# adaLN, S4D convolution and SwiGLU on one core: x normalised once as whole rows, the skip term as a matrix product, a new order of instructions

## The chip, the cores and the metric

The kernel runs on one core of one Trainium2 chip. The metric is the device time of one execution in microseconds (us). The engines are TensorE (PE; its weight loads are listed as PEld), VectorE (DVE), ScalarE (ACT), GpSimd (POOL) and SyncE (SP), which here only issues DMA transfers. SBUF and PSUM are the two on-chip memories; x, the weights and the kernel's scratch tensors lie in DRAM.

## The reference

One sequence x of L = 2048 rows and D = 640 channels passes a modulated block. All numbers are f32.

```python
mod = (silu(c) @ w_mod).reshape(6, 640)          # sa, ca, ga, sb, cb, gb
h = layernorm(x) * (1 + ca) + sa
K[d, l] = 2 * Re(sum_n C[d, n] dt[d] * exp(A[d, n] dt[d] l))     # N = 128
y = irfft(rfft(K, 2L) * rfft(h.T, 2L))[:, :L].T + h * D_skip
x = x + ga * y
h = layernorm(x) * (1 + cb) + sb
x = x + gb * ((silu(h @ w1) * (h @ w3)) @ w2)    # F = 1728
```

## The kernel before, in words

**Work and stages.** The 640 channels are five blocks of 128, numbered 0 to 4, and b is such a block below. For each of them three things are made.

- *The convolution's kernel K.* `gen_tasks` and `gen_chunk` make it in 8 chunks of 16 channels, 40 chunks in all. A chunk takes GpSimd (phases `ph`, three operations on sizes, `yy` and `xx`), ScalarE (sines `tr`, in PSUM), VectorE (five multiplications of `yy` and `xx` with `tr`) and TensorE (64 small products into the PSUM tile `kps`). ScalarE then copies `kps` to `ks` in SBUF. `skip` (L1761) adds D_skip, held in `dsk`, to column 63 of each of the chunk's four groups in `ks`; column 63 is where the time slot t = 0 lies.
- *The input h.* `h_tasks` makes it in four tiles of 128 partitions by 4 rows by 128 channels. `h_load` fetches a tile of x with four DMAs of 64 KB into `xq` (SBUF). `h_norm` (L1639) normalises it with four 128x128 operations, one per row slot, on ScalarE or VectorE, from `xq` into a PSUM bank `hn`. `h_mul` (L1650) multiplies by the row rA and `h_add` (L1654) adds rB, both on VectorE with one 128x512 operation; the first works in place in `hn`, the second writes `hb` (SBUF). `h_store` writes `hb` to the DRAM tensor `hs`, from where `h_fetch` brings it back transposed as `xb`.
- *The spectra.* `first_tasks` is the first stage of the transform: TensorE products `ps`, of `xb` for h and of `ks` for K, copied by ScalarE or VectorE to `sp`. `spectra_tasks` is the second stage: products `fh` and `fk` with the table `wb`, VectorE's complex product `fp`, the first stage back `fz`, copied to `zt` and stored in DRAM as `zd`.

`tail_tasks` follows: the last stage back, x + ga*y, the second LayerNorm, transposes, and the first products `gu` of the feed-forward. `ffn` does the rest of the feed-forward. Its instructions stand outside the plan described below, at lines such as L665 and L841.

**What comes before the blocks** (`early_tasks`, L2000). x is loaded whole, as four tiles `xs` with four DMAs of 320 KB each, and its statistics are taken on ScalarE (sums, squares) or VectorE. The squares are written over `xs`, which nothing needs afterwards. `hscale` makes the reciprocal deviations. The modulations sa, ca and ga are made as rows: five products `mr`, from 960 KB loads of w_mod, are spread over the partitions, copied to three rows `rw`, and folded by two 128x640 operations into rA = (1 + ca)*ga and rB = sa*ga (L2114), so that ga is already in h. Then SP loads the 2 MB table `wb`. sb, cb and gb are made in columns, from five more 960 KB loads of w_mod, `c0` to `c4`, into `xs_w` tiles that share the four buffers of `xs`. Their last product leads to `cols` and to an event called `inv`. At `inv` the buffers `xs` are closed and others opened; the loads of h for blocks 1 to 4 and the second spectra wait for it.

**What sets the order.** The class `Plan` (L168) holds the tasks. Each has an engine (or a choice of two), an assumed duration, the tasks that it waits for, buffers that it takes and gives, and a rank. A list scheduler goes through them with a model of the engines, and where several tasks are ready on one engine, the lowest rank goes first. `RANKS` (L34) is a list of numbers, one for each task up to the last spectra, found by a search that was run beforehand; the tasks of `tail_tasks` have ranks written in the code. The resulting order is then fixed for each engine, so each engine runs its queue in order and a waiting instruction holds up all behind it. The assumed durations therefore decide the order and nothing else. Tasks with `port=True` are placed so that VectorE and GpSimd don't run them side by side; the five multiplications of a chunk, `h_mul` and `h_add` haven't got that mark.

**How to find things in the profile.** Everything that is ordered by the plan has one line there, L157, in which the instruction is recorded; tiles tell the operations apart. The numbers of the tiles are left out, so that `sp<-ps` is any copy of the first stage and `kps<-yy,xx` the products of any chunk.

Of the kernel before, what the change touches and what calls it, by code (L numbers as in the profile page):

```python
# [10 lines left out]
F32 = mybir.dt.float32  # L11
# [7 lines left out]
P = 128  # L19
# [262 lines left out]
class K:  # L282
# [132 lines left out]
    def h_stats(self, xs, b):  # L415
# [10 lines left out]
        def squares(j):  # L426
            s = slice(4 * b + j, 4 * b + j + 1)
            nc.scalar.activation(xs[:, j], xs[:, j], AF.Square, bias=self.h_nm[:, s], accum_out=self.h_ss[:, s])
# [1571 lines left out]
    def early_tasks(self, e):  # L2000
# [122 lines left out]
        def load_w(k):  # L2123
            w[k] = self.mod_load_rows(k, 1)
# [51 lines left out]
```

## Time and profile before

| what | value |
|---|---|
| median of 3 runs | 973.41 us (972.67 to 974.10) |
| profiled execution, its own time | 972.31 us |
| its span, first to last instruction | 970.5 us |
| mean granted TensorE clock | 0.975 of full speed |
| TensorE busy | 859.9 us, 89% of the span, 7985 products |
| VectorE busy | 702.0 us, 72% |
| ScalarE busy | 546.4 us, 56% |
| GpSimd busy | 340.5 us, 35% |
| DMA | 127.31 MB, mean 131 GB/s |

The page of the profile shows one execution. A row of busy tenths divides the span into 40 equal slices, one digit for each: 9 means 90% busy or more. The row GB/s shows what the DMA engines moved in a slice. A group's row has the line, the engine, the operation, "out<-in" by tiles, the shape (partitions x elements) and the count, then the busy time in us, the mean duration in ns, and the idle time of the engine just ahead of such instructions with what ended it. A row of the timeline begins with the start in us from the span's start and the duration in us. A row of windows has the window, its length, and then for PE, PEld, DVE, ACT and POOL the busy time with the number of instructions, the granted clock, the DMA share and the GB/s.

### The profile page before, as it was taken

The page shows a single profiled execution, that of the slowest core. Times are in us where ns is not written, and L with a number is a line of the kernel's source. Part 1 is how long each engine was busy: PE and PEld are TensorE (multiplying, and loading weights), DVE is VectorE, ACT ScalarE, POOL GpSimd, SP SyncE. Part 2 cuts the span into 40 slices and gives each one's busy share as a digit, 9 for nine tenths or more (in the row PEclk, how much of TensorE's full clock was granted, in tenths as well). Part 3 has the DMA queues.
Part 4 walks back from the last instruction along what each step waited for, and adds up shares of the span by engine and source line. Part 5 has one row for each costly group of instructions (what it writes and reads, how often), then busy time and mean ns, then how long its engine had stood idle before and what let it go on. Part 6 is the DMA issues. An engine that isn't in the chain of part 4 may idle for free.

```text
span 970.5 us, 20551 instructions
## 1 busy us (share of the span) xinstructions
PE 859.9 (89%) x7985; PEld 681.8 (70%) x7985; DVE 702.0 (72%) x1395; ACT 546.4 (56%) x1022; POOL 340.5 (35%) x371
## 2 busy tenths in 40 slices
PE   1464787889899997899999999999999999999997
PEld 1132665767778884677777778888788888888775
DVE  7998899999999968886767677557456464645422
ACT  6877788979888851564434455346444344443412
POOL 1797889879799600002111111000011212120000
PEclk9996999999999999799999999999999999999999
DMA  9955453723425268935434422276342322220374
GB/s 218 275 168 191 111 136 95 177 66 106 111 80 152 74 159 206 241 118 182 122 120 139 122 96 68 82 209 194 112 134 64 102 77 86 82 82 28 108 220 133
DMA packets 110506, 127.31 MB, mean 131 GB/s; under 512 B 10568, under 2 KB 90696, under 8 KB 109128
## 3 DMA queue, kind: packets, MB, share of 16 engines
q1 hardware_dynamic: 109032, 125.21, 45.3%
q8 instruction: 63, 1.03, 0.5%
q10 hardware_dynamic: 1376, 0.79, 0.3%
q14 instruction: 35, 0.29, 0.1%
HBM read 95.82 MB, written 30.15 MB: 130 GB/s over the span
## 4 chain that ended last, share of the span: by engine, by line
PE 70%; DVE 17%; ACT 5%; issue 4%; DMA 3%; POOL 1%; SPq 1%; ACTq 0%; DVEq 0%
PE c L157 19%; PE acc L157 18%; PE X L157 12%; PE ps L157 4%; PE gu L157 3%; DVE yy L157 3%; PE kps L157 3%; PE fz L157 2%; PE fk L157 2%; DVE fp L157 2%; PE fh L157 2%; DVE hn L157 2%; DVE xx L157 2%; DVE xb L157 1%; ACT tr L157 1%
## 5 line engine op out<-in xcount | busy, mean ns | idle before, releaser
L157 PE MATMUL acc<-ah,w 128*128 128x512 f32 x560 | 173.2, 395 | 2.4 <-DMA w<-w2d 1.7
L157 PEld LDWEIGHTS acc<-ah,w 128*128 128x128 f32 x560 | 103.7, 188 | 26.4 <-issue 2.1
L157 PE MATMUL acc<-al,w 128*128 128x512 f32 x260 | 102.4, 394 | 0.0
L665 DVE TENSOR_TENSOR wl<-s,wh 128x256 fp32r<-128x256 f32 x92 | 38.9, 423 | 67.5 <-ACT wh L664 67.1
L841 POOL TENSOR_TENSOR s<-wr 128x256 f32<-128x256 f32 x22 | 16.4, 744 | 187.8 <-DMA wr<-in_w 94.8
L157 POOL TENSOR_TENSOR ph<-p,p 128x1024 int32<-128x1024 int32 x40 | 79.2, 1979 | 8.2 <-ACT tr L157 8.0
L664 ACT ACTIVATE wh<-s 128x256 fp32r<-128x256 f32 x92 | 37.6, 410 | 78.5 <-PE X L157 58.1
L157 PE MATMUL kps<-yy,xx 128*32 128x64 f32 x2560 | 51.8, 234 | 28.6 <-DVE xx L157 21.4
L157 DVE TENSOR_TENSOR yy<-yy,tr 128x512 f32<-128x512 f32 (+1 forms) x80 | 75.3, 943 | 1.2 <-ACT tr L157 0.6
L157 PEld LDWEIGHTS kps<-yy,xx 128*32 128x32 f32 x2560 | 45.1, 116 | 38.3 <-issue 22.0
L664 ACT ACTIVATE wh<-wr 128x256 fp32r<-128x256 f32 x92 | 38.4, 418 | 56.0 <-PE X L157 42.3
L842 POOL TENSOR_TENSOR s<-s,wr 128x256 f32<-128x256 f32 x22 | 16.6, 755 | 134.0 <-issue 133.9
L902 ACT ACTIVATE t<-g 128x512 f32<-128x512 f32 x44 | 27.8, 632 | 52.7 <-DVE g L866 52.7
L157 ACT ACTIVATE tr<-ph,hpi 128x512 f32<-128x512 f32 x80 | 54.6, 690 | 4.4 <-DVE xx L157 2.7
L157 PEld LDWEIGHTS acc<-al,w 128*128 128x128 f32 x260 | 48.9, 188 | 10.8 <-DVE al L665 0.3
L871 DVE SCALAR_TENSOR_TENSOR g<-t,g 128x512 f32<-128x512 f32 x48 | 33.7, 702 | 31.3 <-ACT t L902 29.3
L157 POOL TENSOR_TENSOR yy<-e,e 128x512 f32<-128x512 f32 x48 | 52.4, 1109 | 8.8 <-PE kps L157 5.9
L157 DVE TENSOR_TENSOR xx<-tr,xx 128x512 f32<-128x512 f32 x80 | 54.3, 680 | 1.1 <-ACT tr L157 1.1
L157 PE MATMUL ps<-wk,ks 128*64 128x128 f32 x640 | 42.4, 285 | 13.6 <-DVE ks L157 8.9
L157 ACT ACTIVATE tr<-ph 128x512 f32<-128x512 int32 x80 | 47.3, 598 | 12.4 <-DVE yy L157 6.5
L157 PE MATMUL ps<-wk,xb 128*64 128x128 f32 x640 | 46.1, 295 | 6.3 <-ACT sp L157 3.0
L157 PEld LDWEIGHTS ps<-wk,ks 128*64 128x64 f32 x640 | 37.0, 143 | 20.3 <-ACT hn L157 6.6
(448 smaller groups left out, 2379.7 us busy)
## 6 DMA issues: line engine op xcount, KB each, us to landing
w<-w2d SPq DMA_DIRECT2D x42, 640.0 KB, 3.9
wr<-in_w SPq DMA_DIRECT2D x50, 320.0 KB, 3.9
zd<-zt SPq DMA_DIRECT2D x40, 256.0 KB, 2.9
w2d<-w SPq DMA_DIRECT2D x14, 640.0 KB, 3.5
xs<-in_x SPq DMA_DIRECT2D x16, 320.0 KB, 11.3
hs<-hb SPq DMA_DIRECT2D x20, 256.0 KB, 2.5
xb<-hs SPq DMA_DIRECT2D x20, 256.0 KB, 4.9
iz<-zd SPq DMA_DIRECT2D x32, 160.0 KB, 5.0
```

The source lines that it names most:

```text
L157: self.prev = self.k.order(f(*a, **kw), self.prev)
L664: self.nc.scalar.activation(H, v, AF.Copy)
L665: eng.tensor_tensor(Lo, v, H.bitcast(F32), op=ALU.subtract)
L841: eng.tensor_tensor(s[0], u[:, 0:2], u[:, 2:4], op=ALU.add)
L842: eng.tensor_tensor(s[1], s[0], g[:, 0:2], op=ALU.subtract)
L871: V.scalar_tensor_tensor(g, th, 1.0, g, op0=ALU.add, op1=ALU.mult)
L902: tanh = lambda o, i: A.activation(o, i, AF.Tanh, scale=0.5)
```

## The change

- `squares` writes its result to a spare tile `junk`, so that `xs` keeps x.
- New tasks `zn` normalise each of the 16 row slots of `xs` in place, once `hscale` is done, with one 128x640 operation on ScalarE or VectorE (`norm_rows`). Four new DMA tasks `zo` store the four tiles, 1.3 MB each, in a new DRAM tensor `zs`.
- `h_load` of the blocks 1 to 4 fetches its tile from `zs` with one DMA of 256 KB, and waits for its `zo`; block 0 has no load and reads `xs` directly. `h_norm` and its PSUM bank are gone: `h_mul` reads `xq` (block 0: `xs`) and writes `xq`, in SBUF. The buffers of `xs` are given free by `zo` and by `h_mul` of block 0, not by the squares.
- `skip` is gone. After the 64 products of a chunk, one more product, of the 128x128 identity `ident` with the chunk's 128x4 of `dsk`, is added to column 63 of each group of `kps`. The copy to `ks` follows as before. The first stage waits for that copy (`r`) in place of the addition (`d`), and a chunk's products wait for the copy of two chunks before.
- `h_make`, which nothing called, is deleted.
- Many assumed durations are changed, also of tasks in `tail_tasks`, and `RANKS` is new throughout. Some waits for the last of eight tasks are written as waits for all eight.

```diff
+        self.zs = d.tile([4, P, 4, D], F32, name="zs")
...
-            nc.scalar.activation(xs[:, j], xs[:, j], AF.Square, bias=self.h_nm[:, s], accum_out=self.h_ss[:, s])
+            nc.scalar.activation(self.junk, xs[:, j], AF.Square, bias=self.h_nm[:, s], accum_out=self.h_ss[:, s])
...
     def h_load(self, pc, b):
-        t = self.xq0[b] if pc == 0 else self.fpool.tile([P, 512], F32, name=f"xq{pc}{b}", tag="xq", bufs=2)
-        t = t.rearrange("p (j d) -> p j d", j=4)
-        self.x_slots(t, b, pc * P, pc * P + P)
+        t = self.fpool.tile([P, 512], F32, name=f"xq{pc}{b}", tag="xq", bufs=2).rearrange("p (j d) -> p j d", j=4)
+        self.nc.sync.dma_start(t, self.zs[b, :, :, pc * P:pc * P + P])
         self.xq[pc, b] = t
...
+            nc.tensor.matmul(kps.rearrange("p (e b) -> p e b", b=64)[:, :, 63], self.ident, self.dsk[:, d0 // P, d0 % P // 4:d0 % P // 4 + 4],
+                             start=False, stop=True, skip_group_check=True)
...
-    def h_norm(self, pc, b, out, e):
-        x = self.xq[pc, b]
-        self.xq[pc, b] = out = out.rearrange("p (j d) -> p j d", j=4)
+    def norm_rows(self, b, j, e):
+        x = self.xs[b][:, j]
         rstd, nb = self.h_rs
-        for j in range(4):
-            s = slice(4 * b + j, 4 * b + j + 1)
-            if e == "DVE":
-                self.nc.vector.tensor_scalar(out[:, j], x[:, j], rstd[:, s], nb[:, s], op0=ALU.mult, op1=ALU.add)
-            else:
-                self.nc.scalar.activation(out[:, j], x[:, j], AF.Identity, scale=rstd[:, s], bias=nb[:, s])
+        s = slice(4 * b + j, 4 * b + j + 1)
+        if e == "DVE":
+            self.nc.vector.tensor_scalar(x, x, rstd[:, s], nb[:, s], op0=ALU.mult, op1=ALU.add)
+        else:
+            self.nc.scalar.activation(x, x, AF.Identity, scale=rstd[:, s], bias=nb[:, s])
 
     def h_mul(self, pc, b):
-        x = self.xq[pc, b]
-        self.nc.vector.tensor_tensor(x, x, bc(self.rA[:, pc * P:pc * P + P], 1, 4), op=ALU.mult)
+        x = self.xq[pc, b] if pc else self.xs[b][:, :, :P]
+        if pc == 0:
+            self.xq[pc, b] = self.xq0[b].rearrange("p (j d) -> p j d", j=4)
+        self.nc.vector.tensor_tensor(self.xq[pc, b], x, bc(self.rA[:, pc * P:pc * P + P], 1, 4), op=ALU.mult)
...
-            A.activation(self.ks[b][:, 4 * c:4 * c + 4, :], kps[c].rearrange("p (e b) -> p e b", b=64), AF.Copy)
-
-        def skip(c):
-            o = slice(4 * c, 4 * c + 4)
-            V.tensor_add(self.ks[b][:, o, 63], kps.pop(c).rearrange("p (e b) -> p e b", b=64)[:, :, 63], self.dsk[:, b, o])
+            A.activation(self.ks[b][:, 4 * c:4 * c + 4, :], kps.pop(c).rearrange("p (e b) -> p e b", b=64), AF.Copy)
...
-            add(n + "p", "PE", 1.1, lambda c=c: ch[c][4](), [n + f"m{i}" for i in range(5)], t + 3,
+            add(n + "p", "PE", 1.25, lambda c=c: ch[c][4](), [n + f"m{i}" for i in range(5)] + (["dsk"] if b == 0 else []) + ([f"{g}.{c - 2}.r"] if c > 1 else [f"g{b - 1}.{c + 6}.r"] if b else []), t + 3,
...
-            add(n + "d", "DVE", .1, lambda c=c: skip(c), [n + "r"] + (["dsk"] if b == 0 else []), t + 3, give=[("kg", n + "p")])
...
+            room = ["mr0", "mr1"][:2 if i == 3 else 1]
+            if b:
+                add(n + "l", "SP", 0, lambda i=i: self.h_load(b, i), ["inv", f"zo{i}"], t - 8, dma=[262144], take=[("xq", 1)])
+            add(n + "x", "DVE", .61, lambda i=i: self.h_mul(b, i), ["fold"] + ([n + "l"] if b else room + [f"zn{i}{j}" for j in range(4)]), t + .1,
+                give=[] if b else [("xs", f"x{i}")])
+            add(n + "a", "DVE", .61, lambda i=i: self.h_add(b, i), [n + "x"], t + .2, take=[("hz", 1)], give=[("xq", n + "l")] if b else [])
...
+        for b in range(4):
+            for j in range(4):
+                add(f"zn{b}{j}", ("ACT", "DVE"), (.87, .52), lambda e, b=b, j=j: self.norm_rows(b, j, e), ["hscale"], W["h"](0, b) - 1 + .01 * j)
+            add(f"zo{b}", "SP", 0, lambda b=b: nc.sync.dma_start(self.zs[b], xs[b]), [f"zn{b}{j}" for j in range(4)], W["h"](0, b), dma=[327680] * 4, give=[("xs", f"x{b}")])
...
-        add("fold", "DVE", 1.6, fold, [f"rw{g}" for g in range(4)], 22, port=True)
+        add("fold", "DVE", 3.2, fold, [f"rw{g}" for g in range(4)], 22, port=True)
...
-            add(f"c{k}", "SP", 0, lambda k=k: load_w(k), ["x3", "h0.3.l"] + ([f"c{k - 1}"] if k else []), W["col"] + k, dma=[983040], take=[("xs", 1)])
+            add(f"c{k}", "SP", 0, lambda k=k: load_w(k), ["x3"] + ([f"c{k - 1}"] if k else []), W["col"] + k, dma=[983040], take=[("xs", 1)])
```

More of the change, by code (lines that the diff above doesn't have):

```diff
@@ L1169, in lo @@
                     self.low(h[:, :k], l[:, :k], x)
-                add(f"wh{m}.{i}", "ACT", .36, hi, names + (after[i:i + 1] if after else []), rank)
-                add(f"wl{m}.{i}", "DVE", .42, lo, [f"wh{m}.{i}"], rank)
+                add(f"wh{m}.{i}", "ACT", .32, hi, names + (after[i:i + 1] if after else []), rank)
+                add(f"wl{m}.{i}", "DVE", .34, lo, [f"wh{m}.{i}"], rank)
         def down_split(m, rank):
@@ L1613, in border @@
             self.x2 += [self.fp.tile([P, 4, D], F32, name=f"x2{i}") for i in (2, 3)]
-        plan.add("change", None, 0, change, [f"g{b}.7.p", f"g{b}.7.d"] + [f"h{b}.{i}.x" for i in range(4)], 0, own=True)
+        plan.add("change", None, 0, change, [f"g{b}.7.p", f"g{b}.7.r"] + [f"h{b}.{i}.x" for i in range(4)], 0, own=True)
         self.tail_tasks(border, cut)
@@ L1953, in exp_tasks @@
             take=[("xs", 1)] if b == 1 else [])
-        add(f"exp{b}", "ACT", 3.46, exps, [f"al8{b}"] + ([f"g{b - 2}.7.z{i}" for i in range(3)] if b > 1 else ["turn1"] if b else []), t, table="exp",
+        add(f"exp{b}", "ACT", 3.46, exps, [f"al8{b}"] + ([f"g{b - 2}.{c}.z{i}" for c in (5, 6, 7) for i in range(3)] if b > 1 else ["turn1"] if b else []), t, table="exp",
             give=[("xs", f"al8{b}")] if b == 1 else [])
```

82 lines of the change are left out of this document (30 added, 52 removed), and 125 rows, old and new, of the table RANKS.

## The prediction

> **What bounds the kernel now.** I read the page first, its busy shares and slices, for which engine is full and when.
>
> ```profile
> DVE  7998899999999968886767677557456464645422
> ...
> POOL 1797889879799600002111111000011212120000
> ```
>
> A slice is 24.3 us. VectorE (DVE) is at 9 in nearly all of the first 14 slices, GpSimd (POOL) at 7 to 9, and both fall off behind. The windows say how full they are there.
>
> ```profile
> 34.00:336.00 302.00, 240.06 (x4780) 191.75 (x4782) 286.55 (x523) 246.79 (x427) 267.04 (x258) 0.94 0.48 131
> 100.00:345.00 245.00, 213.85 (x4350) 179.13 (x4352) 231.80 (x431) 203.26 (x347) 207.66 (x203) 0.97 0.43 110
> ```
>
> The columns are PE, PE's weight loads, DVE, ACT, POOL. Between 34 and 336 us VectorE idles 15.5 of 302 us and GpSimd 35 us. So VectorE sets the pace of the front part and GpSimd is close behind. TensorE's timeline shows where that part ends.
>
> ```profile
> 345.22 1.17 PE L157 MATMUL kps<-yy,xx 128*32 128x64 f32 x64
> 346.32 3.71 PE L157 MATMUL ps<-wk,ks 128*64 128x128 f32 x64
> ...
> 397.73 0.78 PE L157 MATMUL gu<-x0h,wh_u 128*128 128x512 f32 x1
> ```
>
> 345.22 is the last of the 40 generated chunks. From there TensorE works through the last spectra without VectorE holding it, the feed-forward begins at 397.73, and the 572.8 us from there to the end are code that the diff leaves alone. So I take the change's worth as the shift of that last kps, and a small term behind it. The profiled execution took 972.3 us, 1.8 above its span and 1.1 below the median of the runs, 973.4; the sum is made against 972.3.
>
> **The change part by part.** Prices of what goes, from VectorE's groups by line and shape up to 350 us:
>
> ```profile
> L157 DVE TENSOR_SCALAR hn<-xq,rs_y_h,rs_n_h 128x128 f32<-128x128 f32 x44 | 18.1, 412 | 1.2
> L157 DVE TENSOR_TENSOR hn<-hn,rw 128x512 f32<-128x512 f32 x20 | 13.8, 692 | 0.6 <-ACT hn L157 0.6
> L157 DVE TENSOR_TENSOR hb<-hn,rw 128x512 f32<-128x512 f32 x20 | 13.6, 680 | 0.0
> L157 DVE COPY sp<-ps 128x512 f32<-128x512 f32 x20 | 13.4, 683 | 3.2 <-PE ps L157 3.1
> L157 DVE TENSOR_TENSOR ks<-kps,dsk 128x4 f32<-128x4 f32 x40 | 6.0, 157 | 9.8 <-ACT ks L157 5.6 <-PE kps L157 3.1 <-ACT hn L157 1.1
> ...
> L157 DVE COPY zt<-fz 128x512 f32<-128x512 f32 x5 | 3.4, 684 | 0.8 <-PE fz L157 0.7
> ...
> L157 DVE TENSOR_SCALAR hn<-sp,rs_y_h,rs_n_h 128x128 f32<-128x128 f32 x8 | 3.3, 411 | 0.2
> ```
>
> *Work on VectorE.* 52 block normalisations go: 18.1 + 3.3 = 21.4 us. 40 skip additions go: 6.0 us. In the changed kernel's order of instructions, 8 of the 16 whole-row normalisations stand on VectorE and 8 on ScalarE. None of that kind is in the front part; the feed-forward has one of the same shape:
>
> ```profile
> 392.79 1.12 DVE L157 TENSOR_SCALAR xn<-x,rs_y_n,rs_n_n 128x640 f32<-128x640 f32 x2
> ```
>
> That is 0.56 each, 8 of them 4.5 us. ScalarE loses 28 block normalisations, gains 8 long ones, and with 246.79 of 302 us it wasn't full. The order also moves copies between the two engines: up to the last chunk 6 fewer sp copies stand on VectorE (4.1 us) and 4 more zt copies (2.7), and one more 128x512 and two more 128x128 small operations (1.2 by the rows below). The sum is -21.4 - 6.0 + 4.5 - 0.2 = **-23.1 us**.
>
> *The 40 multiplications and additions that stay.* They are 20 by rA and 20 by rB, and their count doesn't change, but their input does: hn lay in PSUM, and now x and the row lie both in SBUF. What that means beside a busy GpSimd, the timeline shows at the two 128x640 operations that make rA and rB, which have two SBUF inputs:
>
> ```profile
> 67.66 1.07 POOL L157 TENSOR_TENSOR yy<-e,e 128x512 f32<-128x512 f32 x1
> 67.66 1.75 DVE L157 SCALAR_TENSOR_TENSOR rw<-rw,wb 128x640 f32<-128x640 f32 x1
> ...
> 68.68 1.65 POOL L157 TENSOR_TENSOR xx<-e,e 128x512 f32<-128x512 f32 x1
> 69.33 1.68 DVE L157 TENSOR_TENSOR rw<-rw,wb 128x640 f32<-128x640 f32 x1
> 70.29 1.65 POOL L157 TENSOR_TENSOR yy<-e,e 128x512 f32<-128x512 f32 x1
> ```
>
> The first two rows below are two-input operations on SBUF early on, when GpSimd does nothing; the third is a one-input copy, SBUF to SBUF, of which there are four (shortest, median, longest in ns).
>
> ```profile
> 10.25 0.83 DVE L157 TENSOR_TENSOR late<-late,dt 128x640 f32<-128x640 f32 x1 [2.96 <-DMA late<-in_a_im]
> ...
> 12.73 0.68 DVE L157 TENSOR_TENSOR xb<-late 128x512 f32<-128x512 f32 x1
> ```
>
> ```profile
> L157 DVE TENSOR_SCALAR p<-pB x4: 269/289/1078, 32.2 to 155.6; 128x128 int32<-128x128 int32 x4
> ```
>
> The two engines take turns. The 128x640 takes 0.83 alone and 1.68 to 1.75 here, 0.9 more, and GpSimd's operation behind it takes 1.65 in place of 1.07, 0.6 more. The one-input p<-pB can wait as well: 1.08 in place of 0.27. The hn rows above, with a PSUM operand, keep 0.68 to 0.69 all through the busy stretch. So the change trades an operand that never waits for one that does, with no gain when alone (0.68 beside 0.69).
>
> The price of one such wait lies between 0 (GpSimd idle) and the 0.9 of the rw rows. How long GpSimd's instructions are:
>
> ```profile
> L157 POOL TENSOR_TENSOR ph<-p,p 128x1024 int32<-128x1024 int32 x40 | 79.2, 1979 | 8.2 <-ACT tr L157 8.0
> L157 POOL TENSOR_TENSOR yy<-e,e 128x512 f32<-128x512 f32 x48 | 52.4, 1109 | 8.8 <-PE kps L157 5.9 <-DVE fp L157 1.5 <-DVE hn L157 1.4
> ```
>
> By place: the 8 of the first channel block stand close together beside a dense GpSimd, so I take 0.9: 7 us. The order puts all 32 others between the chunks 14 and 21, where VectorE has some 88 us of work and GpSimd some 65 (8 ph, 21 yy and xx, the rest small), so it is busy about 0.74 of the time. An operation that arrives at random then waits 0.74 of about 0.7, the mean rest of an instruction of 1.1 or 1.98: 0.5 each, 17 us. The 8 whole-row normalisations, at the dense place too, I put at 0.6, near the 0.8 of p<-pB: 5 us. Together **+29 us**. The ends are 12 (the first 16 can't miss a dense GpSimd, the 32 may) and 43 (48 at 0.9).
>
> The Trainium skill, "SBUF — State Buffer", section "Who interferes with whom", says which VectorE operations share ports with GpSimd, held for a whole instruction by whoever started first: those with two SBUF inputs beside a GpSimd that reads SBUF, and one-input ones only in a two-port mode. The trace agrees for the first kind at 67.66 and 69.33; whether the 128x640 normalisations run in such a mode no row shows beside a busy GpSimd. If they don't, the 5 us go and the sum below would be 2 in place of 7.
>
> *Waits that go.* VectorE idled 9.8 us ahead of its skip additions, for ScalarE's copy or for kps. In a queue that runs in order the next operation's wait takes part of that place; I take half, **-5 us** (0 to -9.8).
>
> *What GpSimd pays.* Some three quarters of the 48 operations stop it for 0.6: 21 us, against 35 us of idle time. Among the 32 it has room. Ahead of them it has not: the order runs 14 chunks before the first spectra, where the kernel before runs 10, and GpSimd must have made them. I take **+7 us** (0 to +21).
>
> *TensorE* gets 40 skip products of ident by 128x4. Nearest rows:
>
> ```profile
> L157 PEld LDWEIGHTS pv<-ident,mc x8: 186/192/192, 103.5 to 104.3; 128*128 128x128 f32 x8
> L157 PE MATMUL pv<-ident,mc x8: 252/252/273, 103.5 to 104.3; 128*128 128x4 f32 x8
> ```
>
> At most 0.44 each, 18 us, beside 31 us in which TensorE idles between 100 and 345; I cost it at nothing. If that cover is gone it is 5 to 10 us. Behind the last kps the new order leaves three ks products of 0.93 in place of four: **-0.9 us**.
>
> *DMA.* The normalised x goes out in four stores of the size of the loads below, 5.2 MB. SP issues them behind the 2 MB table wb and ahead of the five xs_w loads, whose buffers they free; 16 block loads go at the start, and 64 of 64 KB become 16 of 256 KB, so SP's queue gets shorter.
>
> ```profile
> DMA  9955453723425268935434422276342322220374
> GB/s 218 275 168 191 111 136 95 177 66 106 111 80 152 74 159 206 241 118 182 122 120 139 122 96 68 82 209 194 112 134 64 102 77 86 82 82 28 108 220 133
> ...
> xs<-in_x SPq DMA_DIRECT2D x16, 320.0 KB, 11.3
> ...
> xs_w<-in_w_mod SPq DMA_DIRECT2D x5, 960.0 KB, 8.1
> ```
>
> From the end of the second rw at 71 us, 2.1 + 5.2 + 4.9 + 2 (hs out and back) = 14.3 MB must pass before the columns exist that let the first spectra start. At 218 to 275 GB/s that is 52 to 66 us, until 123 to 137. The 14 chunks in front take until about 143, as the 11th stood at 128 before and the waits of the first 16 come on top:
>
> ```profile
> 128.13 1.15 PE L157 MATMUL kps<-yy,xx 128*32 128x64 f32 x64 [0.36 <-DVE xx L157]
> ```
>
>  So I cost it at nothing; at the third slice's 168 GB/s it would be 85 us, until 156, and then cost 13.
>
> **Sum:** -23.1 + 29 - 5 + 7 - 0.9 = +7.0. 972.3 + 7.0 = 979.3, and 1.1 for the median: **980 us**.
>
> **The rivals.**
>
> *Relief survives (faster).* The condition is that GpSimd idles or runs small operations whenever one of the 32 comes, which the early burst allows, as VectorE has more to do there than GpSimd. Then only the 12 us of the first 16 are left and GpSimd pays nothing: -23.1 + 12 - 5 - 0.9 = -17, so 956 us. For it: GpSimd idles 35 us. Against it: it is busy in 267 of 302 us. 0.30.
>
> *Columns late (much slower).* The stores and the loads behind them get 168 GB/s, the xs_w loads end at 156 and the first spectra wait 13 us; it decides once the rate stays under some 200 GB/s. VectorE has little else then, since the h of all later blocks wait for the same columns (inv). 980 + 13 = 993 us. For it: DMA works at 9 tenths in the first slices. Against it: the rate there reached 275. 0.14.
>
> *Nothing left.* Waits of 29 us with nothing on GpSimd (-23.1 + 29 - 5 - 0.9 = 0): 973 us, within 1.9 us. 0.08. That the order itself isn't better, whatever its durations, lies in the forecast: I give it no gain, as the front part has 15.5 us of VectorE idle to win and no more.
>
> **How the numbers follow.** Forecast (976 to 988) 0.48, relief 0.30, columns 0.14, nothing left 0.08. About 0.2% (1.9 us) is what a measurement can tell from no change. Faster by more: 0.30; within: 0.08; slower: 0.62. The range reaches from 951 (the relief case with all 9.8 us of the skip's waits gone) to 998 (the ceiling of 43 for the waits makes 994.4 and 1.1, 995, and a little of the columns' wait on it); about 0.1 is left on each side.
>
> **What would show it.** Right: the 40 operations with rw take 1.0 to 1.6 us on average in place of 0.69, and GpSimd's yy and xx beside them 1.6; the last kps starts at 350 to 357; 52.5 us from it to the first gu stay. Wrong by the first rival: the 40 stay near 0.75 and the last kps starts at about 329. By the second: TensorE waits on xs_w ahead of its last pm, and the first fh starts after 155. If the time from the last kps to the end moves by over 2 us, the split I made doesn't hold.

## The result, and the profile after

The changed kernel takes 988.18 us (median of 4 runs, 986.73 to 989.87) against 973.75 us before: a ratio of 1.0151, 95% interval 1.0132 to 1.0170, so 14.4 us slower. The forecast was 980, slower, in a range up to 998: the sign and the place were right, and the loss was about twice as large (14.4 us where 6.6 were forecast). The profiled execution took 989.37 us, its span is 987.6, the mean granted clock 0.956 (before 0.975).

TensorE's timeline of the changed kernel (start, duration) shows where the time went:

```profile
365.01 1.17 PE L152 MATMUL kps<-yy,xx 128*32 128x64 f32 x64
...
366.42 1.75 PE L152 MATMUL ps<-wk,ks 128*64 128x128 f32 x28
...
415.46 0.78 PE L152 MATMUL gu<-x0h,wh_u 128*128 128x512 f32 x1
```

The last chunk starts 19.8 us later than before (365.01 against 345.22). From there to the first gu it is 50.5 us (before 52.5), and from gu to the end of the span 572.1 (before 572.8). The two profiled executions differ by 17.1 us; all of this, and 2.7 us more, lies ahead of the last chunk, where the prediction put the loss. Of the page's busy tenths, the rows of VectorE and GpSimd:

```profile
DVE  7899579899979888987676767657464555646322
...
POOL 2798899588988740001211212000022121220000
```

A slice is now 24.7 us. VectorE is at 5 in the fifth slice (99 to 123 us), where it was at 8 before, and GpSimd at 5 in the eighth (173 to 198 us). The windows of both kernels, changed kernel first (columns as in the prediction: PE, PEld, DVE, ACT, POOL, then the granted clock, the DMA share and GB/s):

```profile
34.00:366.00 332.00, 268.22 (x5110) 219.09 (x5110) 291.36 (x451) 253.70 (x429) 279.07 (x254) 0.89 0.45 132
...
66.00:100.00 34.00, 14.12 (x278) 12.30 (x279) 32.04 (x51) 20.61 (x32) 29.10 (x25) 0.53 0.77 288
100.00:130.00 30.00, 18.16 (x345) 12.73 (x339) 18.53 (x24) 23.15 (x34) 26.59 (x28) 0.62 0.46 134
130.00:160.00 30.00, 24.46 (x515) 21.80 (x505) 25.99 (x40) 19.39 (x32) 29.68 (x25) 0.95 0.22 70
160.00:190.00 30.00, 23.50 (x282) 17.79 (x281) 26.45 (x41) 20.44 (x31) 19.07 (x18) 0.82 0.67 182
```

```profile
34.00:346.00 312.00, 250.06 (x5013) 200.45 (x5016) 292.79 (x532) 255.00 (x441) 267.54 (x258) 0.95 0.47 128
...
100.00:130.00 30.00, 24.02 (x512) 20.92 (x512) 27.49 (x54) 22.59 (x41) 23.25 (x25) 0.94 0.48 116
130.00:160.00 30.00, 24.41 (x428) 18.45 (x430) 29.86 (x57) 26.87 (x45) 29.08 (x28) 1.00 0.53 133
160.00:190.00 30.00, 22.19 (x440) 19.21 (x436) 29.20 (x59) 26.32 (x45) 27.31 (x32) 0.94 0.60 151
```

Up to the last chunk VectorE works 291.4 us in place of 292.8, and idles 40.6 in place of 19.2. The 20 us are idle time, +21.4, and the forecast had +2 for it (-5 and +7). Nearly three quarters of it lie between 100 and 190 us: 19.0 us idle against 3.5. From 100 to 160 us GpSimd is nearly full and VectorE idles 15.5 us; its waits there name GpSimd's `yy` and `xx` for 7.5 us, ScalarE for 5.7 and TensorE for 1.8. Then VectorE has the h of the later blocks to make, and GpSimd is the one that idles (160 to 190: 10.9 us, before 2.7). The chunks show the same: the changed kernel's 14th comes a little earlier than before (149.82 us against 153.43), and the 15th long after it (186.57 against 163.26). The products of these two chunks, changed kernel first:

```profile
149.82 1.17 PE L152 MATMUL kps<-yy,xx 128*32 128x64 f32 x64
...
186.57 1.17 PE L152 MATMUL kps<-yy,xx 128*32 128x64 f32 x64
```

```profile
153.43 1.16 PE L157 MATMUL kps<-yy,xx 128*32 128x64 f32 x64 [0.42 <-DVE xx L157]
163.26 1.59 PE L157 MATMUL kps<-yy,xx 128*32 128x64 f32 x64 [2.42 <-ACT sp L157]
```

The waits that the prediction spoke of are there too, and smaller than forecast. VectorE's groups:

```profile
L152 DVE TENSOR_TENSOR xq<-xq,rw 128x512 f32<-128x512 f32 x16 | 19.5, 1220 | 0.4 <-DMA xq<-zs 0.4
...
L152 DVE TENSOR_TENSOR hb<-xq,rw 128x512 f32<-128x512 f32 x16 | 13.9, 876 | 0.0
...
L152 DVE TENSOR_SCALAR xs<-xs,rs_y_h,rs_n_h 128x640 f32<-128x640 f32 x8 | 7.5, 998 | 0.0
...
L152 DVE TENSOR_TENSOR sp<-xs,rw 128x512 f32<-128x512 f32 x4 | 4.1, 1034 | 0.0
...
L152 DVE TENSOR_TENSOR hb<-sp,rw 128x512 f32<-128x512 f32 x4 | 3.1, 800 | 0.0
```

The 40 operations with rw take 40.6 us, 13.2 more than the 27.4 before, and the 8 row normalisations 7.5, 3.0 more than forecast without waits: 16.2 in place of 29. GpSimd's own busy time rose by 11.5 us (267.5 to 279.1 in these windows).

### The profile page after: what moved, and what is told of

The parts are those of the page before. It is cut to its first block, busy times and chain, and to the rows that moved or that the text cites. A ratio compares the mean times of both kernels' runs of the same rounds, so it can differ in the third digit from the quotient of the medians.

```text
span 987.6 us, 20492 instructions
## 1 busy us (share of the span) xinstructions
PE 878.6 (89%) x8065; PEld 699.5 (71%) x8065; DVE 701.1 (71%) x1313; ACT 542.4 (55%) x1003; POOL 354.0 (36%) x368
## 4 chain that ended last, share of the span: by engine, by line
PE 75%; DVE 10%; DMA 4%; ACT 3%; issue 3%; POOL 3%; SPq 1%; ACTq 0%; DVEq 0%; POOLq 0%
PE c L152 19%; PE acc L152 17%; PE X L152 12%; PE ps L152 7%; PE kps L152 5%; PE gu L152 3%; PE fk L152 3%; PE fz L152 3%; PE fh L152 3%; DVE yy L152 2%; DVE fp L152 1%; DMA wk<-in_t_wk 1%; PE iy L152 1%; DVE xx L152 1%; PE tp L152 1%
## 5 line engine op out<-in xcount | busy, mean ns | idle before, releaser
L152 PE MATMUL kps<-yy,xx 128*32 128x64 f32 x2560 | 54.4, 244 | 37.6 <-DVE xx L152 36.4
L646 DVE TENSOR_TENSOR wl<-s,wh 128x256 fp32r<-128x256 f32 x92 | 38.9, 423 | 67.2 <-ACT wh L645 66.8
L152 PEld LDWEIGHTS kps<-yy,xx 128*32 128x32 f32 x2560 | 48.0, 123 | 52.4 <-POOL p L152 24.2
L152 POOL TENSOR_TENSOR yy<-e,e 128x512 f32<-128x512 f32 x48 | 56.1, 1183 | 3.2 <-issue 2.7
L152 PE MATMUL ps<-wk,xb 128*64 128x128 f32 x640 | 48.4, 304 | 2.8 <-issue 2.2
L646 DVE TENSOR_TENSOR wl<-wr,wh 128x256 fp32r<-128x256 f32 x92 | 40.4, 440 | 14.9 <-ACT wh L645 14.8
L152 ACT ACTIVATE sp<-ps 128x512 f32<-128x512 f32 x66 | 39.0, 594 | 21.6 <-PE ps L152 21.0
```

The source lines that it names most:

```text
L152: self.prev = self.k.order(f(*a, **kw), self.prev)
L646: eng.tensor_tensor(Lo, v, H.bitcast(F32), op=ALU.subtract)
```

## The experiments

What must be told apart are four things that came in together: relief (work that goes), waits beside GpSimd, the later columns, and the new order. **Theory A** is that the waits cost, **C** that the columns' lateness costs, **D** that relief on VectorE is worth its time; **B** and **E** are that waits or relief fall into slack, **F** to **I** concern the order. In the texts of the first four runs, Theory 1 stands for D in skip_alone and for A and C together in the others, and Theory 2 says that the new order is what costs. To hold the order still, most kernels replace the planner by a written list of tasks, with which each engine gets its instructions in a chosen order:

```diff
-        self.order = self.place({n: t[4] for n, t in T.items()} | dict(zip(searched, found)))
-        for s, f, e, n in self.order:
+        for x in ORDER.split():
+            i, j = divmod(int(x), 2)
...
```

"Old order" is that of the kernel before: tasks that both kernels have keep its sequence on every engine, and a task is moved only if something that it waits for comes later. All runs, with the ratio to the runs of the kernel before on the same chip, and the start of the last copy of `kps` to `ks` in ScalarE's timeline (346.4 us before; it comes from one profiled execution, which lies up to 4 us off its median):

| run | median us | ratio | 95% interval | last ks |
|---|---|---|---|---|
| changed kernel | 988.18 | 1.0151 | 1.0132 to 1.0170 | 366.5 |
| skip_alone | 971.37 | 0.9990 | 0.9971 to 1.0010 | 348.1 |
| relief_only | 967.19 | 0.9945 | 0.9917 to 0.9973 | 340.7 |
| sbuf_alone | 1007.55 | 1.0358 | 1.0332 to 1.0383 | 383.1 |
| new_work_old_order | 1003.38 | 1.0313 | 1.0280 to 1.0345 | 378.7 |
| late_cols_old_order | 997.07 | 1.0242 | 1.0218 to 1.0267 | 372.0 |
| early_cols_old_order | 984.20 | 1.0115 | 1.0077 to 1.0153 | 358.8 |
| early_half_psum | 978.60 | 1.0061 | 1.0036 to 1.0086 | 353.8 |
| early_cols_psum_old_order | 977.53 | 1.0039 | 1.0024 to 1.0055 | 351.0 |
| early_psum_spread0 | 980.61 | 1.0083 | 1.0054 to 1.0113 | 357.7 |
| early_sbuf_spread | 981.11 | 1.0089 | 1.0061 to 1.0117 | 357.8 |
| early_psum_spread | 989.69 | 1.0189 | 1.0158 to 1.0219 | 361.4 |
| old_work_new_order | 1009.78 | 1.0375 | 1.0335 to 1.0415 | 384.6 |
| psum_new_order | 995.33 | 1.0231 | 1.0188 to 1.0275 | 368.8 |
| after_half_psum | 991.98 | 1.0204 | 1.0171 to 1.0237 | 368.1 |
| after_add_forward | 989.27 | 1.0174 | 1.0143 to 1.0205 | 364.2 |
| skip_searched | 992.31 | 1.0198 | 1.0177 to 1.0219 | 369.4 |
| early_psum_searched | 991.13 | 1.0189 | 1.0171 to 1.0207 | 365.5 |
| early_cols_searched | 995.88 | 1.0235 | 1.0213 to 1.0256 | 372.6 |

### Relief

**skip_alone** does the skip term's part of the change in the kernel before:

```diff
+            nc.tensor.matmul(kps.rearrange("p (e b) -> p e b", b=64)[:, :, 63], self.ident, self.dsk[:, d0 // P, d0 % P // 4:d0 % P // 4 + 4],
+                             start=False, stop=True, skip_group_check=True)
...
-            add(n + "d", "DVE", .1, lambda c=c: skip(c), [n + "r"] + (["dsk"] if b == 0 else []), t + 3, give=[("kg", n + "p")])
```

> The kernel before, in its own order on every engine, with one part of the change: the skip term is added by TensorE's product into kps, and the 40 additions on VectorE are gone. Theory 1 (VectorE's work and its waits set the front part): 6.0 us of work and a part of the 9.8 us of waits ahead of these additions go, so 960 to 967 us, and the last kps starts 6 to 13 us before 345. Rival (another engine, GpSimd with its 267 of 302 us, takes the place at once): within 2 us of 973.7.

No difference that can be measured; the rival holds. Two rows of VectorE's timeline before show a part of the reason:

```profile
206.35 0.15 DVE L157 TENSOR_TENSOR ks<-kps,dsk 128x4 f32<-128x4 f32 x1
206.42 0.67 DVE L157 TENSOR_TENSOR yy<-yy,tr 128x512 f32<-128x512 f32 x1
```

The next operation starts 0.07 us after the addition, not 0.15: its record overlaps the next one's, so the records' sum of 6.0 us overstates what the 40 of them hold the queue for. And the relief became idle time: in this window of skip_alone VectorE works 4.5 us less than the 292.8 before, and idles that much more:

```profile
34.00:346.00 312.00, 260.53 (x5030) 209.33 (x5032) 288.25 (x493) 253.58 (x440) 267.53 (x258) 0.94 0.47 128
```

**relief_only** takes away all that the change takes away, the skip additions as in skip_alone and the block normalisations:

```diff
-        for j in range(4):
-            s = slice(4 * b + j, 4 * b + j + 1)
-            if e == "DVE":
-                self.nc.vector.tensor_scalar(out[:, j], x[:, j], rstd[:, s], nb[:, s], op0=ALU.mult, op1=ALU.add)
...
+        if e == "DVE":
+            self.nc.vector.tensor_copy(out, x)
+        else:
+            self.nc.scalar.activation(out, x, AF.Copy)
```

> Everything that the change takes away and nothing that it adds, in the order of the kernel before: the skip term is added by TensorE, and each tile's four normalisations (128x128) are replaced by one copy (128x512) to the same PSUM bank on the same engine. It leaves the normalisation of the first LayerNorm out. VectorE has 6.0 + 21.4 - 8.9 = 18.5 us less to do, ScalarE some 9 us less. Theory D (VectorE's work sets the front part, as the prediction had it): 955 to 962 us. Rival E (in a fixed order VectorE's relief turns into idle time, as the 6 us of the skip additions did): 968 us or more.

5.4 us come back (2.6 to 8.1 by the interval), of 18.5: neither theory's number. Up to the last chunk VectorE works 15.3 us less than the 292.8 before, not 18.5:

```profile
34.00:341.00 307.00, 261.27 (x5112) 209.72 (x5114) 277.45 (x454) 246.55 (x424) 268.63 (x258) 0.96 0.48 131
```

So in this fixed order about a third of VectorE's relief turned into time, and D fails in its size.

### The waits beside GpSimd

**sbuf_alone** leaves the kernel before its work and its order, but not the PSUM bank:

```diff
-        self.xq[pc, b] = out = out.rearrange("p (j d) -> p j d", j=4)
+        out = x
...
-            add(n + "n", ("ACT", "DVE"), (1.95, .85), lambda e, i=i, place=place: self.h_norm(b, i, place(), e), [n + "l", "hscale"], t, take=[(bank, 1)],
-                give=[("xq", n + "l")] if b else [])
+            add(n + "n", ("ACT", "DVE"), (1.95, .85), lambda e, i=i: self.h_norm(b, i, None, e), [n + "l", "hscale"], t)
```

> The kernel before with its own work and its own order on VectorE, ScalarE, TensorE and GpSimd, but the normalised tile stays in SBUF (in place in xq) instead of going to a PSUM bank, so that the 40 multiplications and additions have two SBUF inputs. Theory A (waits beside GpSimd are on the path, as the prediction had it): the 40 take 10 to 20 us more than 27.4, GpSimd's yy and xx beside them wait too, and the kernel takes 983 to 1000 us. Rival B (these waits fall into slack, as the 6 us of the skip additions did): within 4 us of the kernel before.

34.9 us slower by the ratio (1.0358 of 973.4), beyond theory A's range. VectorE's groups of this run:

```profile
L157 DVE TENSOR_SCALAR xq<-xq,rs_y_h,rs_n_h 128x128 f32<-128x128 f32 x44 | 32.1, 792 | 3.3 <-DMA xq<-in_x 3.3
...
L157 DVE TENSOR_TENSOR xq<-xq,rw 128x512 f32<-128x512 f32 x16 | 17.5, 1094 | 1.5 <-ACT xq L157 1.5
...
L157 DVE TENSOR_TENSOR hb<-xq,rw 128x512 f32<-128x512 f32 x16 | 14.2, 884 | 0.0
...
L157 DVE TENSOR_SCALAR sp<-sp,rs_y_h,rs_n_h 128x128 f32<-128x128 f32 x8 | 6.8, 910 | 0.0
...
L157 DVE TENSOR_TENSOR hb<-sp,rw 128x512 f32<-128x512 f32 x4 | 3.9, 979 | 0.0
...
L157 DVE TENSOR_TENSOR sp<-sp,rw 128x512 f32<-128x512 f32 x4 | 3.7, 924 | 0.0
```

The 40 two-input operations take 39.3 us, 11.9 more than in PSUM; the 52 one-input normalisations 38.9, 17.5 more. That is 29.4 us more on VectorE, and the last copy to ks comes 36.7 us later. The 34.9 us are not VectorE's alone: GpSimd's same 258 instructions take 278.7 us in place of 267.5, and VectorE waits 3.3 us for loads, whose buffers `xq` the edit holds until the addition. So the run shows that waits beside GpSimd reach the time, where relief did so by a third; it doesn't show how much of the 34.9 each engine's share is. The shortest, the median and the longest of the one-input operation show both faces of SBUF (in ns; the kernel before first, with its PSUM output):

```profile
L157 DVE TENSOR_SCALAR hn<-xq,rs_y_h,rs_n_h x44: 401/414/415, 110.8 to 240.0; 128x128 f32<-128x128 f32 x44
...
L157 DVE TENSOR_SCALAR xq<-xq,rs_y_h,rs_n_h x44: 331/504/2052, 118.4 to 272.3; 128x128 f32<-128x128 f32 x44
```

At its shortest it is faster than with a PSUM output (331 against 401), and in this run, with GpSimd busy 279 of 349 us, it can take 2 us. By the rule of the Trainium skill that the prediction weighed ("SBUF — State Buffer", section "Who interferes with whom"), a one-input operation meets GpSimd only in a two-port mode. These rows agree with such a mode for f32 from SBUF to SBUF; 2052 ns is the longest that was measured.

In the changed work, four runs with early columns (below) take the waits out wholly or by half. **early_half_psum** adds no operation; only the product goes to a bank:

```diff
-        if pc == 0:
-            self.xq[pc, b] = self.xq0[b].rearrange("p (j d) -> p j d", j=4)
+        self.xq[pc, b] = out.rearrange("p (j d) -> p j d", j=4)
```

> The changed work with early columns in the order of the kernel before (984.2 us), with one operand moved: the multiplication writes its product to a PSUM bank instead of SBUF, so the 20 additions have one SBUF input; no operation is added. With early columns alone these 20 additions took 22.8 us, in the kernel before 13.6. Theory A (the waits beside GpSimd are on the path): 9 us of VectorE come back, and the time falls by 5 to 12 us, to 972 to 979. Rival B (slack): within 3 us of 984.2.

5.3 us less than early columns alone by the ratios, within theory A's range, though the two intervals overlap at their ends. The 20 additions went from 17.6 + 5.2 us

```profile
L155 DVE TENSOR_TENSOR hb<-xq,rw 128x512 f32<-128x512 f32 x16 | 17.6, 1097 | 0.1
...
L155 DVE TENSOR_TENSOR hb<-sp,rw 128x512 f32<-128x512 f32 x4 | 5.2, 1296 | 0.0
```

with early columns alone to 13.6 in this run:

```profile
L155 DVE TENSOR_TENSOR hb<-hn,rw 128x512 f32<-128x512 f32 x20 | 13.6, 681 | 0.1
```

**early_cols_psum_old_order** takes out all 40, at the price of 20 copies by ScalarE:

```diff
+    def h_copy(self, pc, b, out, e):
+        x = self.xq[pc, b] if pc else self.xs[b][:, :, :P]
+        self.xq[pc, b] = out = out.rearrange("p (j d) -> p j d", j=4)
...
+            self.nc.scalar.activation(out, x, AF.Copy)
```

> The run with early columns in the order of the kernel before, and beside that ScalarE copies each tile to a PSUM bank ahead of the multiplication, so that none of the 40 operations has two SBUF inputs. Theory A: 10 to 20 us less than early columns alone, 945 to 965 us. Rival B (the waits fall into slack): within 4 us of early columns alone.

6.7 us less than early columns alone, the intervals apart: the direction is theory A's, the size less. VectorE then waited 7.8 us for these copies:

```profile
L156 DVE TENSOR_TENSOR hn<-hn,rw 128x512 f32<-128x512 f32 x20 | 13.9, 696 | 7.8 <-ACT hn L156 7.8
```

So of the 16.1 us by which the 40 operations got shorter (43.7 to 27.6), 7.8 turned into waiting for the copies. Its 16 row normalisations stood as one block of 6.6 us on each of two engines, with a chunk behind them (the fourth copy to ks at 81.3 us, before 75.2). Three runs tried to mend that by placing them apart, one with the copies earlier as well, one without copies. The sequence of tasks on VectorE (the first of the three; in the other two the pairs of zn stand three and four instructions later; `zn` is a row normalisation, m a multiplication of a chunk):

```diff
-fold, zn (8 of them), g0.3.m3, g0.3.m4, h0.0.x
+fold, g0.3.m3, zn12, zn13, g0.3.m4, h0.0.x, ..., h0.0.a, g0.4.m3, zn22, zn23
```

> The run with early columns and PSUM banks in the order of the kernel before (977.5 us), with two placements mended that its trace shows: the 16 row normalisations, which stood as one block of 6.6 us on VectorE and on ScalarE from 67 to 77 us with a chunk behind them (the fourth copy to ks at 81.3 us, in the kernel before at 75.2), are spread over the places of the old ones, 12 on ScalarE and 4 on VectorE; and ScalarE's copies to PSUM stand 12 places of the plan earlier, as VectorE waited 7.8 us for them. Theory I (the remainder of the loss is such placement): 966 to 972 us, at or below the kernel before. Rival: 975 us or more.

> As the run with both placements mended, but the copies to PSUM stay in their places. Theory I: 968 to 975 us, between that run and 977.5.

> As the run with the spread normalisations and the copies in their places, but without copies: multiplication and addition take the rows from SBUF, as the changed kernel does. Theory A (waits beside GpSimd cost): 5 to 12 us more than the run with PSUM banks. Rival B: within 3 us of it.

All three missed their theories' ranges. The first took 989.7 us, which wasn't traced further; the others 980.6 and 981.1, above the 977.5 that they started from. Theory I isn't borne out: these placements didn't help. Nor did the copies make a difference between the last two, as Rival B has it. But VectorE waited as long for them as its 40 operations got shorter (14.6 us, 42.2 without copies and 27.6 with them):

```profile
L156 DVE TENSOR_TENSOR hn<-hn,rw 128x512 f32<-128x512 f32 x20 | 13.9, 697 | 14.7 <-ACT hn L156 14.7
```

So this pair doesn't tell whether the waits beside GpSimd fall into slack; it put another wait in their place. Taking them out of the changed work brought 5 to 7 us where VectorE didn't have to wait as much for the copies.

### The columns

> The changed kernel's operations, all of them, put in the order of the kernel before on every engine; the new row normalisations and stores stand right behind the fold of rA and rB. Theory 1 (the new work costs: operations with two SBUF inputs wait beside GpSimd, and the columns come later because x must be stored before their loads): 983 to 995 us, no better than the changed kernel's 988.2. Theory 2 (the new order costs, the work itself saves): 958 to 970 us.

1003.4 us, worse than in its own order and above Theory 1's range. Two rows of the waits from 60 to 130 us, TensorE's and VectorE's, show why this run alone doesn't tell what it was meant to:

```profile
PE pm L155 <- DMA xs_w<-in_w_mod: 38.5, 3, 32.6
```

```profile
DVE yy L155 <- ACT tr L155: 20.8, 1, 20.8
```

In the old order the columns' products stand early in TensorE's queue. Their loads must wait now for the stores of x, and the chunks behind them wait too. **late_cols_old_order** puts these products behind the chunks; **early_cols_old_order** gives the loads other room, so that they need not wait for the stores:

```diff
+        self.wc = [spf[:, 2048:3968], wbf[:, :1920], wbf[:, 2048:3968]]
...
-        w = self.wm[k] if half == 0 else self.xsp.tile([P, 4 * D], F32, name=f"xs_w{k}", tag="xs", bufs=4)[:, :3 * D]
+        w = self.wm[k] if half == 0 else self.wc[k] if k < 3 else self.xsp.tile([P, 4 * D], F32, name=f"xs_w{k}", tag="xs", bufs=4)[:, :3 * D]
...
-        add("wb", "SP", 0, lambda: nc.sync.dma_start(self.wb, self.t_wb), ["fold", "mr4", "lat1", "turn1"], 60, dma=[2097152])
+        add("wb", "SP", 0, lambda: nc.sync.dma_start(self.wb, self.t_wb), ["mc1", "mc2"], 60, dma=[2097152])
```

> The changed kernel's work in the order of the kernel before, with the columns as late as the stores make them, but their products placed on TensorE behind the chunks for which they stood in the way (in the run without this TensorE waited 38.5 us for xs_w with chunks behind it). Theory C: the first fh comes at about 145 and the kernel takes 985 to 995 us, 10 to 25 us more than with early columns. Rival A: within 5 us of the run with early columns.

> The changed kernel's work in the order of the kernel before, and the columns' loads no longer wait for x to be stored: the first three go to parts of sp and wb that are idle at that time, the last two to xs as before, and the table wb follows them. Theory C (what the change costs is that the columns come 40 us later, which puts off the first spectra and every h of blocks 1 to 4): 960 to 980 us against 1003 without this, the first fh at 125 to 132. Rival A (the waits beside GpSimd cost it): still 985 or more.

997.1 with late columns, 984.2 with early ones: 12.9 us, and 19.2 against the run with TensorE's queue blocked; the intervals lie apart. Both lie above theory C's ranges for them. The first fh of the four kernels, in this order: before, changed, late columns, early columns:

```profile
123.72 1.13 PE L157 MATMUL fh<-sp,wb 128*64 128x128 f32 x16
```

```profile
145.05 1.13 PE L152 MATMUL fh<-sp,wb 128*64 128x128 f32 x16
```

```profile
136.09 1.13 PE L155 MATMUL fh<-sp,wb 128*64 128x128 f32 x16
```

```profile
128.38 1.14 PE L155 MATMUL fh<-sp,wb 128*64 128x128 f32 x16
```

In the old order theory C's difference holds: 12.9 us, in its 10 to 25. The first fh with late columns came at 136 and not at 145, and TensorE's granted clock differs too (0.77 from 100 to 130 us with late columns, 0.88 with early ones), which this pair can't take apart. Rival A also has its part, as early columns alone still lose 1.2%.

### The new order

> The kernel before, its operations unchanged, put in the order of the changed kernel on every engine: the loads of the first block and its block normalisations stand just ahead of their multiplications, the skip additions just behind their copies. Theory 2 (the new order costs): slower than the changed kernel, as VectorE has some 20 us more to do in the same order: 995 to 1010 us. Theory 1 (the new work costs): near the kernel before, 970 to 980 us.

1009.8: the new order is 37 us worse for the old work, as Theory 2 had it, while the old order is no better for the new work, as Theory 1 had it. For that it is 15 us worse than the new one (1003.4 against 988.2; 9 with the products mended). So each order is fitted to its own work, and "the new order costs" was the wrong question. The next three kernels keep the new order and change one thing each.

> The changed kernel in its own order, but ScalarE first copies each fetched tile (128x512) from SBUF to a PSUM bank, and the multiplication and the addition work there, as in the kernel before; 20 more ScalarE operations of about 0.6 us, none of VectorE's has two SBUF inputs among the 40. In the changed kernel the 40 take 40.6 us, in the kernel before 27.4. Theory 1 (the waits beside GpSimd are what costs): these 13 us come back on VectorE and 6 or more of GpSimd's with them, so 968 to 976 us. Theory 2 (the order costs): at most 4 us come back, 984 to 988 us, or it is slower for the banks.

> The changed kernel in its own order, with the product of the multiplication in a PSUM bank instead of SBUF and nothing else changed. Its 20 additions took 17.0 us, in the kernel before 13.6. Theory A: 3 to 6 us less than 988.2, 982 to 985. Rival B: within 2 us of 988.2, or above it where the banks run short.

Both became slower than the changed kernel, by 7 and by 4 us, outside the ranges of theories 1 and A, although the waits went: the additions took 13.6 in place of 17.0 us in the second. In the first the 40 took 13.1 us less (40.6 to 27.5), and VectorE waited 13.8 us for ScalarE's copies:

```profile
L156 DVE TENSOR_TENSOR hn<-hn,rw 128x512 f32<-128x512 f32 x20 | 13.9, 698 | 14.2 <-ACT hn L156 13.8
```

The banks, too, are shared with the spectra; whether that slowed the second, which has no copies, isn't settled.

The last edit in the new order, as the sequence of tasks on VectorE:

```diff
 h0.3.x, g0.5.m3, g0.5.m4, g0.6.m1, ..., g0.7.m2
+h0.3.a
 g0.7.m0, al81, g0.7.m1, ..., g1.0.m3
-h0.3.a
```

> The changed kernel in its own order, with one step of it moved: the addition of rB to the first block's last tile stands right behind that tile's multiplication on VectorE (in the changed kernel 25 us behind it, at 115.6 us), and its store with it on SP's queue, so that the columns' third load no longer waits behind that store from 94.9 to 116.8 us. The columns should be done at 115 to 122 us instead of 142. Theory F (with the order of everything else fixed, earlier columns find no use: the chunks and VectorE's queue are laid out for late ones): within 4 us of 988.2. Rival C (the columns' lateness itself is what the changed kernel waits for): 10 us or more below it, 978 or less.

The addition came forward by 11 of the 19 instructions behind its multiplication and not by all, as its buffer in the ring hz is free no earlier; it ran at 100.1 us in place of 115.6. The time stayed (989.3), as theory F says. But the columns didn't come earlier, and there my expectation was wrong. SP's queue of the changed kernel has the gap that I meant to close (start, duration):

```profile
92.52 2.36 SPq L152 DMA_DIRECT2D xs_w<-in_w_mod  x1
116.75 0.36 SPq L152 DMA_DIRECT2D hs<-hb  x1
117.17 0.50 SPq L152 DMA_DIRECT2D xs_w<-in_w_mod  x1
```

It closed: all five loads were issued by 109 us, in place of 122. The last columns' products ran at 140.36 all the same, against 141.76:

```profile
140.36 1.06 PE L155 MATMUL pm<-xs_w,sc 128*32 128x512 f32 x8
```

They stand behind chunks and first-stage products in TensorE's queue. So in this order, which was searched for the work with late columns, their earlier loads changed nothing; rival C, which needs earlier columns, wasn't put to the test.

Three more runs searched an order anew, with the durations of the traces, for the skip term alone, for early columns with PSUM banks and for early columns alone.

> The kernel before with the skip term on TensorE, as in the run of that part alone (971.4 us), but its order up to the first feed-forward products searched anew for this work, with the durations that the traces show (GpSimd's 2.0 and 1.09 us among them). Theory G (relief turns into time once the order is fitted to it): 952 to 966 us. Rival H (the order was no obstacle, or the planner's model is too far from the chip for such a search to show): 968 us or more.

> The changed kernel's work with the two remedies, early columns and the copies to PSUM banks (977.5 us in the order of the kernel before), in an order searched anew for it. Theory G: 955 to 970 us, below the kernel before. Rival H: 972 us or more.

> The changed kernel's work with early columns alone (984.2 us in the order of the kernel before), its operations with two SBUF inputs kept, in an order searched anew with 1.1 and 0.9 us for them as traced. Theory A (the waits beside GpSimd cost in any order): 970 to 985 us, 5 to 15 us above the run with PSUM banks and a searched order. Rival (once the order expects them, these waits cost nothing): within 4 us of that run.

They took 992.3, 991.1 and 995.9 us, slower than the same work in the old order (971.4, 977.5, 984.2). In these orders some part of the output is made from other data than the reference's, probably since a wait is missing in the list of tasks; which one wasn't traced. They tell nothing of the theories, only that an order which is good by the planner's model can be some 20 us slower on the chip.

## Why the prediction was right in direction and wrong in size

- **Where:** right in the main. All of the loss is ahead of the last chunk. But the last kps started at 365, not at 350 to 357, and the time from there to the end fell by 2.7 us where 0.9 was forecast; that is over the 2 us that were set as the limit for this split.
- **The sum:** it had VectorE's work at +5.9 us (-23.1 and +29) and its idle time at +2 (-5 and +7). Measured up to the last chunk are -1.4 and +21.4. So the step that failed is the one that left the idle time nearly as it was: "VectorE sets the pace of the front part". Part of the error was hidden, as the work came out 7.3 us below the forecast.
- **The relief, -23.1 us:** the instructions went, but the prices were sums of records that overlap, and taking away a like amount in a fixed order gave 5.4 us. VectorE idled only 15.5 of 302 us, but it is tied in each chunk to ScalarE, TensorE and GpSimd, and time taken from it turned into waiting for them.
- **The waits, +29:** the mechanism is shown (sbuf_alone), the size was too large. The 40 took 1.01 us on average, at the lower end of the 1.0 to 1.6 named as the sign, and the 16 additions after xq 0.88. The normalisations waited 0.4 each, not 0.6. Together 16.2.
- **"Waits that go", -5, and "what GpSimd pays", +7:** these were mis-sized. Measured is +21.4 us of idle time on VectorE, of which 15.6 between 100 and 190 us.
- **DMA, "So I cost it at nothing":** this term failed with it. The time of the columns was about as forecast (the last product at 141.8, the first fh at 145; 13 chunks stand ahead of it, not 14), and TensorE never waited for xs_w there. But I priced the lateness as a wait at the first fh. The runs point to another price: until the columns exist nothing of the later blocks' h and no second spectra can be made, so the order has only chunks to offer, and in them GpSimd is nearly full and VectorE not. What is left over is made up later, when GpSimd idles. Early against late columns are worth 12.9 us in the old order. That the 21.4 us in the changed kernel's own order come from this fits its windows and wasn't isolated.
- **The rivals:** "relief survives" is refuted. "Columns late" was named with the wrong sign to look for (a wait on xs_w, fh after 155), and its price, 13 us, is what the pair of runs gave in another order, by another way; that the two numbers agree is luck.
- **TensorE, at nothing:** no cost of the skip products shows in the old order, as skip_alone is no slower. What TensorE's lower clock cost in the changed kernel wasn't in the sum and wasn't tried (last section).
- **Slips:** the range's 995 adds the 1.1 for the median twice, as 994.4 has it already. GpSimd is at 7 to 9 in twelve of the first 14 slices; the first has 1 and the last 6.

In the old order, with TensorE's queue mended, the new work loses 23.6 us (2.42%), and the parts can be set side by side by the ratios: late columns 12.4 us, the waits of the additions 5.3, those of the multiplications less ScalarE's copies 2.1 (the intervals overlap, so it may be nothing), and 3.8 that nothing here explains. In the changed kernel's own order they can't be separated, since every edit there moved the time by some us for reasons of its own; how its 14.4 us divide into columns, waits and clock stays open. None of these versions beats the kernel before by more than a measurement can tell; relief_only does, but leaves a LayerNorm's work out.

## What to carry to other kernels

Before an operand moves from PSUM to SBUF to save work, look at who else uses SBUF at that time: in the old order, taking these waits out of the changed work gave 5 to 7 us, as much as all the work that was saved had been worth there (5.4). When a change makes a buffer free later, ask what can't be started until then, and which engine has work in the meantime; the price need not be a wait for that buffer, it can be two engines that are full one after the other instead of side by side. Don't count relief on the busiest engine as time won in an order that was searched for other work: here a third of it came through. And when a copy or a bank is put in to mend a wait, look whether the engine now waits for that instead.

## What the runs showed of the hardware that was not expected

- A one-input f32 operation (128x128) took 331 ns at best from SBUF to SBUF and up to 2052 with GpSimd busy, and 401 to 415 from SBUF to PSUM (sbuf_alone, before).
- TensorE's granted clock fell further in the changed kernel: 0.53 from 66 to 100 us and 0.62 from 100 to 130, where it had been 0.70 and 0.94. The columns' products show it: two of the three from 100 to 130 us took 1.93, and those behind took 1.06, as here:

```profile
127.28 1.93 PE L152 MATMUL pm<-xs_w,sc 128*32 128x512 f32 x8
...
136.51 1.06 PE L152 MATMUL pm<-xs_w,sc 128*32 128x512 f32 x8
```

So does a chunk's kps (before, 1.96 at 92.68 and 1.15 at 95.79):

```profile
113.04 1.96 PE L152 MATMUL kps<-yy,xx 128*32 128x64 f32 x64 [7.10 <-DVE xx L152]
...
135.11 1.16 PE L152 MATMUL kps<-yy,xx 128*32 128x64 f32 x64
```

In these stretches TensorE is busy 14 of 34 and 18 of 30 us; its busy share alone doesn't order the clocks, as it was busy 12 of 34 us before, at 0.70. In the chain of work that ended last, kps, ps and pm fill 64.5% of the stretch from 90 to 146 us, where they filled 34.8% before. Set against the durations of the same groups at the higher clock, those on the chain ahead of 130 us took some 8 us longer, and some 2 before. That is an estimate from these rows, and it makes the clock a rival for a part of the loss; whether it adds to the loss or only follows from it was not tried.
